# An attention and two gated token-mixing blocks on one core: the planner's constants, its choice rule, buffer counts, and one operation of a decode

## The chip, the cores and the metric

The kernel runs on one core of a Trainium2 chip. The metric is the device time of one execution in microseconds (us). Three runs of the kernel before are given; the profile is of a further execution, with its own time.

## The reference

Three stages follow each other for each of 4 batches (sequence 768, model width 384).

- Attention: 8 heads of width 48. A state of 48x48 per head is multiplied by a gate `f` (a sigmoid of `f_logit`) and takes the outer product of `k` and `v` at each of the 768 tokens; `q` reads it.
- Block 1: `h = gelu(x @ w_in)` with 1024 columns, split in `u` and `v`; `v` is normalised over its columns and scaled by `g_ln`, mixed over the tokens (`w_sg @ v_n + b_sg`), multiplied by `u`, and `x + gated @ w_out` comes out.
- Block 2: `theta = x @ w_theta`; `x cos(theta)` and `x sin(theta)` are mixed over the tokens by `w_tok_r` and `w_tok_i` and added to `x`, which gives `y`; the output is `y + max(y @ w_ch, 0)`.

The weights `w_in`, `w_out`, `w_theta`, `w_tok_r`, `w_tok_i` and `w_ch` arrive as 64-bit floats; `w_sg` and the rest as 32-bit floats.

## The kernel before, in words

**Matmuls.** Every product of block 1 and block 2 is made of three matmuls (`mm3`, L794 to L796): each fp32 operand is split into a high part in the fp32r type and a remainder, and high*high, high*low and low*high are accumulated in one bank of PSUM. `split`, `xsplit` and `load_split` make the parts: ScalarE copies the value into the high part (L803, L813, L454), and VectorE subtracts (L804, L814, L455). Four banks (`mm`) serve the products, two double banks (`at`) the attention.

**Order of the stages.** The attention of batch 0 comes first, in two halves, with nothing dense to run beside it; TensorE is given multiplications with the identity (L1041) to fill its idle time there. Then block 1 of the batches 0 to 3 follows, each beside the attention of the next batch, and then block 2 of batch 3, 0, 1 and 2. In block 1, `p3` mixes over the tokens in all four banks at once (L794 to L796 on `st` and `ar`); at its end VectorE takes the four banks out (L857), multiplies with `u` (L862) and splits.

**The decode (`load_f32`, L417 to L444).** A weight tile of 64-bit floats is loaded as pairs of 32-bit words: into a `raw` buffer (L428) if it is in the background, into an `st` buffer otherwise. ScalarE takes the absolute value of the upper words into a `dt` buffer (L440). VectorE takes the maximum with `TINY` (L441), shifts left by 3 and masks (L442), puts sign and top exponent bit back from the upper word (L443) and the upper bits of the lower word in (L444). `load_split` then splits the `dt` tile: into `win` and `wout`, into `st`, or into a `wt` buffer (L454, L455). 46 tiles are decoded: 12 of `w_in` (256 columns), 4 of `w_out`, and 30 in the background: 24 of `w_tok_r` and `w_tok_i`, 3 of `w_theta`, 3 of `w_ch` (384 columns each). From `wt` a tile is written to a scratch tensor in device memory (L494; L478 for the last six), from which the token-mixing weights are streamed into `st` for each batch (L504, 384 KB) and the channel weights are loaded in one piece into `win` (L486, 1152 KB). A `raw` buffer is free when L444 of its tile is done, a `wt` buffer when its write has landed.

**The attention's output** is copied from PSUM by ScalarE (L744), sent by DMA into `xst` (L767) in pieces of up to 72 KB, and split from there (L813, L814).

**The planner.** All instructions of the main program are put in order before the kernel is built (`Plan.schedule`). Each operation has a due time, a duration and its dependencies; the due time of what feeds it is lowered accordingly (`cost`). The planner then runs a list schedule over the five engines: for each engine it takes the earliest time at which an operation of it could start, looks at all that could start within `LOOK` of that, and picks the one that is due first. Before, a start that was later by some us put `STALL` times as much on its due time. A DMA that is issued at some time is taken to begin moving `ISSUED` later, to move at `RATE` bytes per us behind the DMAs before it, and to have landed `LANDED` after that; the next is not issued until the modelled queue is at most `BACKLOG` us long. The picked order is the order of the instructions on each engine. On the chip each engine runs its instructions in that order, and waits where the data or the buffer isn't there. All DMAs of the main program are issued from SP, in order.

Of the kernel before, what the change touches and what calls it, by code (L numbers as in the profile page):

```python
# [8 lines left out]
F32 = mybir.dt.float32  # L9
# [3 lines left out]
AF = mybir.ActivationFunctionType  # L13
ALU = mybir.AluOpType
# [17 lines left out]
MAGIC = 12582912.0  # L32
TWO_PI = 6.283185
MIN_DECAY = 2.0**-58
TINY = 2.0**-15

N_F = 1
N_SEED = 1
# [8 lines left out]
N_U = 4  # L47
WARM_TO = 100.0
WARM_GAP = 0.3
N_W = 4  # L50
N_DT = 3
N_RAW = 2
N_EARLY = 8
LATE_AT = -6.0
LATE_STEP = 3.3
N_MM = 4
GROUPS0 = [(p, p + 1) for p in range(NP)]
GROUPS1 = GROUPS0
LEAD = 2.0
LATE = 30.0  # L60
HF0, HF1, V_AT, U_AT, DENSE = (-60.0, -40.0), (-25.0, -10.0), -35.0, -27.0, -33.0
ATT_FROM = 0.0
ATT_TO = 100.0
PACE = 1.0
YQ = "SP"
LOOK = 0.15
STALL = 15.0
SWITCH = 2.0
WAIT2 = 0.065

TICK = 10.24 / 3
DMA_SLACK = 1.0
BACKLOG = 2.5
ISSUED = 1.2
LANDED = 0.6
RATE = 335e3
DRAIN = {"PE": 0.0, "DVE": 0.12, "ACT": 0.14, "POOL": 0.05, "SP": 0.0}
LAT = {"PE": 0.21, "DVE": 0.13, "ACT": 0.145, "POOL": 0.1, "SP": 0.0}
SETS = {"G": "gelu_apprx_tanh_and_others", "L": "natural_log_exp_and_others", "S": "silu_and_others"}
# [2 lines left out]
def lat(a, b):  # L82
    if a == b:
        return 0.0
    return 0.21 if a == "PE" else LAT[a] + (0.1 if b == "PE" else 0.0)
# [35 lines left out]
class Plan:  # L121
# [58 lines left out]
    def schedule(self):  # L180
        for o in reversed(self.ops):
            cost = LAT[o.eng] + o.dur + ((ISSUED + LANDED + o.dma / RATE) * DMA_SLACK if o.dma else 0.0)
            for d in o.succ:
# [4 lines left out]
        table, dev, lands = None, 0.0, []  # L188
# [6 lines left out]
        def slot_time(o):  # L195
            t, taken = 0.0, {}
            for b in o.need:
                if b.held:
                    continue
                s = b.slots  # L200
                mine = taken.setdefault(id(s), [])
                at = s.next + len(mine)
                if at >= len(s.order) or s.order[at] is not b:
                    return None
                best = None
                for i in range(s.n):
                    if i in mine:
                        continue
                    prev = s.owner[i]
                    u = 0.0  # L210
                    if prev is not None:
                        for a in prev.acc:
                            if a.end is None:
                                u = None
                                break
                            u = max(u, a.end + (0.0 if a.dma else lat(a.eng, o.eng)))
                    if u is not None and (best is None or u < best[0]):
                        best = (u, i)
                if best is None:
                    return None  # L220
                b.slot = best[1]
                mine.append(best[1])
                t = max(t, best[0])
            return t

        def run(a, dur, left):

            c, i = left / dur, int(a / TICK + 1e-9)
            while left > 1e-6:
                rate = c if ticks.get(i - 1, 0) >= 3060 else c / 2  # L230
                n = min(left, rate * ((i + 1) * TICK - a))
                ticks[i] = ticks.get(i, 0) + n
                left, a, i = left - n, a + n / rate, i + 1
            return a
# [4 lines left out]
        while todo:  # L239
            pick = None  # L240
            for e, c in cand.items():
                best = None
                ready = []
                for o in c:
                    t = o.est
                    if o.need:
                        u = slot_time(o)
                        if u is None:
                            continue
                        t = max(t, u)  # L250
                    t = max(t, free[e])
                    if o.dma and e != "POOL":
                        t = max(t, dev - BACKLOG, lands[-8] if len(lands) >= 8 else 0.0)
                    ready.append((t, o))
                if not ready:
                    continue
                t0 = min(x[0] for x in ready)
                for t, o in ready:
                    if t > t0 + LOOK:
                        continue  # L260
                    vt = o.vt + (SWITCH if self.loads(o, table) else 0.0) + (t - t0) * STALL
                    if best is None or (vt, o.n) < best[0]:
                        best = ((vt, o.n), t, o)
                if pick is None or best[1] < pick[0]:
                    pick = (best[1], best[2])
            t, o = pick
            todo -= 1
            cand[o.eng].remove(o)
            o.need = [b for b in o.need if not b.held]
            for b in o.need:  # L270
                b.held = True
                b.slots.owner[b.slot] = b
                b.slots.next += 1
            if o.eng == "PE" and self.idle and t < WARM_TO and self.quiet(free["PE"]) is not None:
                n, a, bank = 0, free["PE"], self.quiet(free["PE"])
                while True:
                    old = dict(ticks)
                    e = run(a, 0.2145, 512)
                    if e > t - WARM_GAP:
                        ticks.clear()  # L280
                        ticks.update(old)
                        break
                    n, a = n + 1, e
                if n and bank is not None:
                    out.append(((n, bank), None))
            o.start = t
            load, dur = self.loads(o, table), o.dur
            if load:
                table = load
                dur += 1.3  # L290
            if o.eng == "PE":
                dur = run(t, dur, o.cols) - t
            free[o.eng] = o.end = t + dur
            if o.dma:
                dev = max(dev, o.start + ISSUED) + o.dma / RATE
                o.end = dev + LANDED
                if o.eng != "POOL":
                    lands.append(o.end)
            out.append((o, load))
            for d in o.succ:  # L300
                d.left -= 1
                wait = 0.0 if o.dma else lat(o.eng, d.eng) if o.eng != d.eng else DRAIN[o.eng] if o in d.made else 0.0
                d.est = max(d.est, o.end + wait)
                if d.left == 0:
                    cand[d.eng].append(d)
# [27 lines left out]
def body(tc, ctx, att, qkv, flog, w_in, g_ln, w_sgT, b_sg, w_out, w_theta, w_rT, w_iT, w_ch, out):  # L333
    nc = tc.nc
# [41 lines left out]
    def make_state(attention):  # L376
        g = State()
        g.st = Slots(main, "st", N_ST)
        g.w32, g.raw = Slots(main, "wt", N_W), Slots(main, "raw", N_RAW)
        g.dt = Slots(main, "dt", N_DT)  # L380
        g.tmp = Slots(main, "tmp", N_TMP)
# [26 lines left out]
    def dma(pl, eng, nbytes, fn, r=(), w=(), wp=(), vt=None):  # L408
        pl.op(eng, {"SP": 0.43, "ACT": 0.66, "POOL": 1.05}[eng], fn, r, w, wp, dma=nbytes, vt=vt)

    def v2(n):
        return 0.065 + n * 0.00053

    def v1(n):
        return 0.069 + n * 0.00104

    def a1(n):  # L417
        return 0.1 + n * 0.00081

    def load_f32(pl, g, d, src, vt, background=False):  # L420

        n = src.shape[-1]
        get = lambda: d.t[:, :n]
        if src.dtype != I64:
            dma(pl, "SP", n * 512, lambda: nc.sync.dma_start(get(), src), w=[d], vt=vt - 3)
            return
        raw = pl.buf(g.raw if background else g.st, [P, 2 * TH], I32)
        dma(pl, "SP", n * 1024, lambda: nc.sync.dma_start(raw.t[:, : 2 * n], src.bitcast(I32)), [], [raw], vt=vt - 3)  # L428

        def bits():  # L430
            r = raw.t[:, : 2 * n].rearrange("p (n two) -> p n two", two=2)
            return r[:, :, 0], r[:, :, 1]

        def op(dur, fn, eng="DVE"):
            pl.op(eng, dur, fn, [raw], [d], vt=vt)

        V, iget = nc.vector, lambda: get().bitcast(I32)


        op(a1(n), lambda: nc.scalar.activation(get(), bits()[1].bitcast(F32), AF.Abs), "ACT")  # L440
        op(v2(n), lambda: V.tensor_scalar(get(), get(), TINY, None, ALU.max))  # L441
        op(v2(n), lambda: V.tensor_scalar(iget(), iget(), 3, 0x3FFFFFFF, ALU.logical_shift_left, ALU.bitwise_and))  # L442
        op(v1(n), lambda: V.scalar_tensor_tensor(iget(), bits()[1], -0x40000000, iget(), ALU.bitwise_and, ALU.bitwise_or))  # L443
        op(v1(n), lambda: V.scalar_tensor_tensor(iget(), bits()[0], 29, iget(), ALU.logical_shift_right, ALU.bitwise_or))  # L444
# [599 lines left out]
    with tc.manual_schedule():  # L1044
# [19 lines left out]
        def blocks(b, x):  # L1064
            get = lambda pl, i: stream(pl, g, i, pl.vt - LEAD, b == 0 and i < 2 * NS)
            return moe(pl, g, x, get, lambda pl, i: mids[i], out[b], PACE, b == 0)
# [24 lines left out]
        for b in (last, *range(last)):  # L1091
            if b != last:
                x = []
                for hf in range(2):
                    t = pl.buf(g.xst[hf], [P, NK, TH])
# [155 lines left out]
```

## Time and profile before

| | us |
|---|---|
| three runs | 653.91, 655.98, 657.85 |
| median | 655.98 |
| the profiled execution | 658.03 |
| its span, first to last instruction | 656.2 |
| its mean granted clock of TensorE | 0.989 |

The span is what the trace shows; 1.8 us of the profiled execution lie around it. A row of a view of groups ends with the busy time and the mean duration of one instruction. A row of the timeline gives start, duration, engine, line, what it writes and reads, and in brackets how long the engine was idle before it and for whom. The chain of waits is followed back from the last instruction and then printed in order of time.

### The profile page before, as it was taken

The numbers are of one execution on the slowest core, as the hardware profiler recorded it, in microseconds if no ns is written. First come the engines' busy times: TensorE is split into PE (matmuls) and PEld (weight loads), VectorE is DVE, ScalarE is ACT, GpSimd is POOL, SyncE is SP. The second block draws the span as 40 slices with busy tenths as digits, with TensorE's granted clock in tenths as the row PEclk, the third lists the DMA queues.
The fourth block names the chain that finished last, engine by engine and source line by source line (L and its number), as shares of the span: only waits on it lengthen the run. The fifth ranks groups of instructions, "written<-read, shape, count | busy, mean of one in ns | idle before, by whom it ended". The sixth has DMA issues, their size and how long they took to land.

```text
span 656.2 us, 15080 instructions
## 1 busy us (share of the span) xinstructions
PE 616.3 (94%) x6033; PEld 572.8 (87%) x6033; DVE 440.7 (67%) x1030; ACT 353.9 (54%) x752; POOL 20.1 (3%) x32
## 2 busy tenths in 40 slices
PE   9897998798999999999999996989999999999996
PEld 8796887777898888898889996889989999998995
DVE  6898888879878989688786768910771284149203
ACT  6658796656894748954477336700570173029100
POOL 2000010000100001000000000000000000000000
PEclk9997999899999999999999999999999999999998
DMA  9621865387447686483885794298538745860852
GB/s 327 213 92 49 282 223 197 92 295 249 150 144 231 230 267 214 133 262 129 258 287 172 267 311 166 77 333 249 180 112 264 241 133 187 247 204 12 272 186 77
DMA packets 55728, 131.50 MB, mean 200 GB/s; under 512 B 6880, under 2 KB 23264, under 8 KB 55648
## 3 DMA queue, kind: packets, MB, share of 16 engines
q1 hardware_dynamic: 55648, 130.45, 60.1%
q8 instruction: 49, 0.80, 0.5%
q14 instruction: 31, 0.25, 0.1%
HBM read 100.93 MB, written 24.77 MB: 192 GB/s over the span
## 4 chain that ended last, share of the span: by engine, by line
PE 57%; ACT 13%; DMA 13%; DVE 12%; issue 3%; SPq 1%; POOL 0%; ACTq 0%; DVEq 0%; POOLq 0%
PE mm L794 16%; PE mm L796 15%; PE mm L795 15%; DMA xst<-y 3%; PE mm L1041 3%; DMA raw<-in_w_rT 2%; ACT ar L803 2%; DMA raw<-in_w_iT 2%; PE at L733 2%; PE at L651 2%; DMA st<-scratch 2%; DMA scratch<-st 1%; PE at L715 1%; PE at L660 1%; DVE dt L443 1%
## 5 line engine op out<-in xcount | busy, mean ns | idle before, releaser
L794 PE MATMUL mm<-st,ar 128*128 128x384 f32 x480 | 164.1, 342 | 2.3 <-DMA st<-scratch 2.3
L795 PE MATMUL mm<-st,ar 128*128 128x384 f32 x480 | 160.7, 335 | 0.7 <-DVE st L455 0.6
L796 PE MATMUL mm<-st,ar 128*128 128x384 f32 x480 | 160.6, 335 | 0.0
L813 ACT CAST x<-xst 128x384 fp32r<-128x384 f32 x72 | 36.7, 513 | 164.7 <-DVE xst L818 126.8
L818 DVE TENSOR_TENSOR xst<-xst,mm 128x384 f32<-128x384 f32 x48 | 25.9, 552 | 115.9 <-PE mm L796 103.6
L794 PEld LDWEIGHTS mm<-st,ar 128*128 128x128 f32 x480 | 90.1, 188 | 5.3 <-issue 2.6
L795 PEld LDWEIGHTS mm<-st,ar 128*128 128x128 f32 x480 | 90.2, 188 | 1.4 <-DVE st L455 1.4
L796 PEld LDWEIGHTS mm<-st,ar 128*128 128x128 f32 x480 | 90.1, 188 | 0.0
L794 PE MATMUL mm<-x,win 128*128 128x384 f32 x168 | 59.2, 353 | 5.8 <-ACT win L454 4.6
L794 PE MATMUL mm<-win,x 128*128 128x512 f32 (+1 forms) x144 | 56.0, 389 | 8.5 <-DVE tmp L857 3.6
L796 PE MATMUL mm<-x,win 128*128 128x384 f32 x168 | 57.1, 340 | 0.0
L795 PE MATMUL mm<-x,win 128*128 128x384 f32 x168 | 57.0, 339 | 0.0
L796 PE MATMUL mm<-win,x 128*128 128x512 f32 (+1 forms) x144 | 52.7, 366 | 0.0
L795 PE MATMUL mm<-win,x 128*128 128x512 f32 (+1 forms) x144 | 52.6, 365 | 0.0
L803 ACT CAST ar<-tmp 128x384 fp32r<-128x384 f32 x80 | 37.7, 509 | 10.7 <-DVE tmp L862 10.2
L814 DVE TENSOR_TENSOR x<-xst,x 128x384 fp32r<-128x384 f32 x72 | 37.4, 552 | 7.9 <-ACT x L813 6.6
L804 DVE TENSOR_TENSOR ar<-tmp,ar 128x384 fp32r<-128x384 f32 x80 | 41.0, 553 | 0.8 <-ACT ar L803 0.5
L794 PEld LDWEIGHTS mm<-win,x 128*128 128x128 f32 x144 | 27.1, 188 | 14.4 <-DVE tmp L857 5.1
L794 PEld LDWEIGHTS mm<-x,win 128*128 128x128 f32 x168 | 32.2, 192 | 7.1 <-ACT win L454 4.7
L794 PE MATMUL mm<-ar,wout 128*128 128x384 f32 x96 | 34.7, 361 | 3.6 <-ACT u L839 1.9
L1041 PE MATMUL mm<-ident 128*128 128x128 f32 x256 | 34.5, 292 | 1.6 <-POOL ident masks.py:199 1.6
L1041 PEld LDWEIGHTS mm<-ident 128*128 128x128 f32 x256 | 32.4, 205 | 2.2 <-POOL ident masks.py:199 1.6
(137 smaller groups left out, 1153.7 us busy)
## 6 DMA issues: line engine op xcount, KB each, us to landing
st<-scratch SPq DMA_DIRECT2D x132, 384.0 KB, 3.7
qkv<-in_qkv SPq DMA_DIRECT2D x28, 536.0 KB, 4.9
scratch<-wt SPq DMA_DIRECT2D x30, 384.0 KB, 3.7
f<-in_flog SPq DMA_DIRECT2D x6, 768.0 KB, 4.5
scratch<-st SPq DMA_DIRECT2D x12, 384.0 KB, 4.1
raw<-in_w_rT SPq DMA_DIRECT2D x12, 384.0 KB, 3.6
raw<-in_w_iT SPq DMA_DIRECT2D x12, 384.0 KB, 3.7
out<-xst SPq DMA_DIRECT2D x24, 192.0 KB, 1.9
```

What stands on the lines that cost most here:

```text
L443: op(v1(n), lambda: V.scalar_tensor_tensor(iget(), bits()[1], -0x40000000, iget(), ALU.bitwise_and, ALU.bitwise_or))
L651: nc.tensor.matmul(U(c, wide[j]), kt.t[wide[a], i * P + HP * j : i * P + HP * (j + 1)], t.t[wide[a], o : o + D], start=True, stop=True)
L733: nc.tensor.matmul((score if own else apart)(a if own else j, i)[rows[j]], S[c][0]()[rows[j]], Q()[rows[j], tok(i, a)], start=False, stop= ...
L794: nc.tensor.matmul(o, h0, h1, start=start, stop=False)
L795: nc.tensor.matmul(o, h0, l1, start=False, stop=False)
L796: nc.tensor.matmul(o, l0, h1, start=False, stop=stop)
L803: pl.op("ACT", a1(n), lambda: nc.scalar.copy(tiles()[0], src.t[:, :n]), [src], [hi])
L804: pl.op("DVE", v1(n), lambda: V.tensor_sub(tiles()[1], src.t[:, :n], tiles()[0].bitcast(F32)), [src, hi], [lo])
L813: pl.op("ACT", a1(TH), lambda: nc.scalar.copy(X[hf][:, 0, k], T()), [src], [hi])
L814: pl.op("DVE", v1(TH), lambda: V.tensor_sub(X[hf][:, 1, k], T(), X[hf][:, 0, k].bitcast(F32)), [src, hi], [lo])
L818: pl.op("DVE", v1(TH), lambda: V.tensor_add(T(), T(), ps.t[:, :TH]), [ps], [xst[hf].parts[k]])
L1041: nc.tensor.matmul(g.mm.tiles[i][:, :P], ident, ident, start=True, stop=True)
```

## The change

- `RATE`, `ISSUED` and `LANDED` change: a transfer of 384 KB (393,216 bytes) is taken to land after 2.1 + 1.25 + 0.5 = 3.85 us, before after 1.2 + 1.17 + 0.6 = 2.97 us.
[...]
- `STALL` goes, and `LOOK` goes from 0.15 to 0.05 us.
- `wt` buffers go from 4 to 2, `dt` from 3 to 5, `raw` from 2 to 3.
- `LEAD`, by which the due time of a streamed tile lies ahead of its use, goes from 2 to 4 us.

```diff
--- before.py
+++ after.py
@@ -32,7 +32,7 @@
 MAGIC = 12582912.0
 TWO_PI = 6.283185
 MIN_DECAY = 2.0**-58
-TINY = 2.0**-15
+TINY = 2.0**-112
 
 N_F = 1
 N_SEED = 1
@@ -47,33 +47,32 @@
 N_U = 4
 WARM_TO = 100.0
 WARM_GAP = 0.3
-N_W = 4
-N_DT = 3
-N_RAW = 2
+N_W = 2
+N_DT = 5
+N_RAW = 3
 N_EARLY = 8
 LATE_AT = -6.0
 LATE_STEP = 3.3
 N_MM = 4
 GROUPS0 = [(p, p + 1) for p in range(NP)]
 GROUPS1 = GROUPS0
-LEAD = 2.0
+LEAD = 4.0
 LATE = 30.0
 HF0, HF1, V_AT, U_AT, DENSE = (-60.0, -40.0), (-25.0, -10.0), -35.0, -27.0, -33.0
 ATT_FROM = 0.0
 ATT_TO = 100.0
 PACE = 1.0
 YQ = "SP"
-LOOK = 0.15
-STALL = 15.0
+LOOK = 0.05
 SWITCH = 2.0
 WAIT2 = 0.065
 
 TICK = 10.24 / 3
 DMA_SLACK = 1.0
 BACKLOG = 2.5
-ISSUED = 1.2
-LANDED = 0.6
-RATE = 335e3
+ISSUED = 2.1
+LANDED = 0.5
+RATE = 315e3
 DRAIN = {"PE": 0.0, "DVE": 0.12, "ACT": 0.14, "POOL": 0.05, "SP": 0.0}
 LAT = {"PE": 0.21, "DVE": 0.13, "ACT": 0.145, "POOL": 0.1, "SP": 0.0}
 SETS = {"G": "gelu_apprx_tanh_and_others", "L": "natural_log_exp_and_others", "S": "silu_and_others"}
@@ -258,7 +257,7 @@
                 for t, o in ready:
                     if t > t0 + LOOK:
                         continue
-                    vt = o.vt + (SWITCH if self.loads(o, table) else 0.0) + (t - t0) * STALL
+                    vt = o.vt + (SWITCH if self.loads(o, table) else 0.0)
                     if best is None or (vt, o.n) < best[0]:
                         best = ((vt, o.n), t, o)
                 if pick is None or best[1] < pick[0]:
@@ -437,8 +436,7 @@
         V, iget = nc.vector, lambda: get().bitcast(I32)
 
 
-        op(a1(n), lambda: nc.scalar.activation(get(), bits()[1].bitcast(F32), AF.Abs), "ACT")
-        op(v2(n), lambda: V.tensor_scalar(get(), get(), TINY, None, ALU.max))
+        op(a1(n) + 0.03, lambda: nc.scalar.activation(get(), bits()[1].bitcast(F32), AF.Abs, scale=TINY), "ACT")
         op(v2(n), lambda: V.tensor_scalar(iget(), iget(), 3, 0x3FFFFFFF, ALU.logical_shift_left, ALU.bitwise_and))
         op(v1(n), lambda: V.scalar_tensor_tensor(iget(), bits()[1], -0x40000000, iget(), ALU.bitwise_and, ALU.bitwise_or))
         op(v1(n), lambda: V.scalar_tensor_tensor(iget(), bits()[0], 29, iget(), ALU.logical_shift_right, ALU.bitwise_or))
```

## Rows read from the trace of the kernel before

**Rows 1.** Stages: length, busy time and count by engine, TensorE clock, DMA share, GB/s.

```profile
0.00:80.00 80.00, 71.27 (x1092) 64.49 (x1093) 66.67 (x199) 56.58 (x127) 7.07 (x20) 0.96 0.57 197
80.00:440.00 360.00, 337.31 (x3744) 304.75 (x3743) 283.44 (x652) 227.04 (x476) 13.00 (x12) 1.00 0.64 212
440.00:656.00 216.00, 207.69 (x1199) 203.58 (x1198) 90.61 (x180) 70.24 (x150) 0.00 (x0) 0.99 0.57 182
```

**Rows 2.** The first stage, line L1041 alone: the fillers on TensorE.

```profile
0.00:80.00 80.00, 34.46 (x256) 32.41 (x256) 0.96 0.57 197
```

**Rows 3.** Timeline of TensorE: the waits that the sum uses.

```profile
119.49 0.69 PE L794 MATMUL mm<-ar,wout 128*128 128x384 f32 x1 [1.93 <-ACT u L839]
332.85 0.50 PE L794 MATMUL mm<-win,x 128*128 128x512 f32 x1 [1.01 <-DVE tmp L857]
369.64 0.44 PE L794 MATMUL mm<-x,win 128*128 128x384 f32 x1 [1.21 <-DVE tmp L857]
396.97 0.41 PE L794 MATMUL mm<-win,x 128*128 128x384 f32 x1 [2.06 <-issue]
438.55 0.41 PE L794 MATMUL mm<-st,ar 128*128 128x384 f32 x1 [2.31 <-DMA st<-scratch]
```

**Rows 4.** Stages within the start, columns as above.

```profile
36.00:52.00 16.00, 15.64 (x245) 13.71 (x245) 15.75 (x52) 7.97 (x21) 0.00 (x0) 1.00 0.35 114
52.00:61.00 9.00, 4.44 (x62) 3.53 (x62) 7.28 (x29) 8.80 (x22) 0.57 (x1) 0.83 0.09 31
```

**Rows 5.** Timeline of VectorE in the start: the last three maxima there.

```profile
61.49 0.90 DVE L441 TENSOR_SCALAR dt<-dt 128x256 f32<-128x256 f32 x3
```

**Rows 6.** VectorE's maximum at 384 columns: busy and mean, idle before it.

```profile
L441 DVE TENSOR_SCALAR dt<-dt 128x384 f32<-128x384 f32 x34 | 11.8, 355 | 12.8 <-ACT dt L440 12.8
```

**Rows 7.** ScalarE by line: no scale, a scale, a scale and a bias tile.

```profile
L904 ACT ACTIVATE tmp<-tmp 128x384 f32<-128x384 f32 x24 | 12.5, 522 | 1.9 <-DVE tmp L902 1.9
L906 ACT ACTIVATE tmp<-tmp 128x384 f32<-128x384 f32 x24 | 12.6, 525 | 0.7
L905 ACT ACTIVATE tmp<-tmp,halfpi 128x384 f32<-128x384 f32 x24 | 14.5, 602 | 0.0
```

**Rows 8.** The chain of waits where raw loads come late: start, us, what.

```profile
323.80 5.39 DMA raw<-in_w_rT
...
361.50 6.14 DMA raw<-in_w_iT
...
389.74 4.59 DMA raw<-in_w_ch
...
395.78 0.56 DVE dt L443
396.34 2.11 DVE tmp L857 x4
```

**Rows 9.** Timeline of ScalarE: the wait ahead of the table load.

```profile
113.86 0.51 ACT L813 CAST x<-xst 128x384 fp32r<-128x384 f32 x1 [2.74 <-DMA xst<-y]
```

**Rows 10.** The view of DMA issues: count, KB each, median us to landing.

```profile
xst<-y SPq DMA_DIRECT2D x48, 72.0 KB, 3.6
```

**Rows 11.** All loads into the raw tiles.

```profile
DMA to landing us min/median/max: 2.9/4.0/8.8
```

**Rows 12.** Waits of SP's queue: for whom, us in total, times, longest.

```profile
SPq L504 <- PE mm L796: 161.3, 114, 13.7
SPq L428 <- DVE dt L444: 55.7, 24, 7.9
```

**Rows 13.** Timeline of SP's queue: the last raw loads, and the weights' load.

```profile
392.29 0.33 SPq L428 DMA_DIRECT2D raw<-in_w_ch  x1
...
403.19 0.33 SPq L428 DMA_DIRECT2D raw<-in_w_ch  x1
...
430.11 0.59 SPq L486 DMA_DIRECT2D win<-scratch  x1
```

**Rows 14.** Timeline of ScalarE: casts into the wt buffers, closest together.

```profile
224.47 1.34 ACT L454 CAST wt<-dt 128x384 fp32r<-128x384 f32 x3
```

## The prediction

> **What bounds the kernel now.** I read the stages first. TensorE is busy for 337.3 of the 360 us between 80 and 440, and for 207.7 of the last 216 [rows 1]; VectorE there for 283.4 and 90.6. So from 80 us on TensorE is the bound, and all that an edit of the order can win there is its idle time: 22.7 us up to 440, and 8.3 behind, most of it the tail behind the last matmul. The first 80 us are another regime: TensorE looks busy for 71.3 us, but 34.5 of them are fillers [rows 2], so its own work is 36.8 us and 43 us are lost to what it waits for.
>
> Then I looked for what ends TensorE's waits. In the start it is VectorE: 15.75 busy of the 16 us from 36 to 52 [rows 4]. From 52 to 61 it is ScalarE, with 8.80 of 9. After 80 us the waits are single ones of 1 to 2.3 us [rows 3]. The chain of waits says what stands behind three of them: in each, VectorE reached L857, which frees TensorE's four banks, late, because a decode stood in front of it whose raw load had landed late [rows 8]. VectorE waited 12.8 us in all for ScalarE's first step of a decode [rows 6]. The fourth, 1.93 us at 119.49, stands behind a table load on ScalarE, and ScalarE had waited 2.74 us for a piece of attention output [rows 9]. The fifth is a stream that came late at 438.55.
>
> **The change part by part.**
>
> *The maximum.* 46 instructions of L441 go, 34 of them at 0.355 us [rows 6]; the 12 of `w_in` run in the start, where three in a series took 0.90 us [rows 5], so 0.30 each. Of the 12, six lie in the stretch from 36 to 52 us, where VectorE has no gap [rows 4]. In a series the next one overlaps the end of the last, so I take 0.22 for each of these, 1.3 us. Three lie beside ScalarE's stretch from 52 to 61 and are hidden by it. The last three at 61.49 stand before the last parts of `w_in`, but ScalarE feeds them one by one, so I take 0.5 of the 0.90. Sum 1.8 us; the bounds are 0 (ScalarE or the transfers take over at once) and 12 x 0.30 = 3.6. The other 34 run after 80 us, where VectorE is idle for 76.6 of 360 us [rows 1]: each is hidden unless it stands directly before L857; those three are counted below. If this cover were gone, they would be worth 34 x 0.355 = 12.1 us.
>
> *The scale on ScalarE.* 46 instructions get a constant factor. L906, with one, takes 525 ns where L904 takes 522 without [rows 7]: 46 x 3 ns = 0.1 us, off the path. The bounds are 0 and 46 x 80 = 3.7 us, the price of L905, which has a bias tile too; I take the near row, as the change adds no tile.
>
> *The transfer times.* A load of a `raw` tile was planned at 2.97 us (1.2 + 0.6 + 393,216/335,000) and took 5.39, 6.14 and 4.59 before the three waits [rows 8]. It is now planned at 2.1 + 0.5 + 1.25 = 3.85, so the planner places ScalarE's and VectorE's steps 0.88 later, and puts something else in front. The step L441 in the same chains gives 0.36 more. That is 1.24 for each wait, and no more than the wait itself: 1.01 of 1.01, 1.21 of 1.21, 1.24 of 2.06 [rows 3], together 3.5 us. The bounds are 0 and 4.3. A piece of attention output was planned at 1.2 + 0.6 + 0.22 = 2.02 us and took 3.6 [rows 10]; it is now planned at 2.83, so 0.81 of the 1.93 us at 119.49 goes, between 0 and 1.93. All these are waits of engines that run in order: behind L440 ScalarE's casts are queued, behind L441 all of VectorE, and for both TensorE waits.
>
> *The buffers.* The third load of `w_ch` was issued at 403.19, where the second had gone at 392.29 [rows 13]. It waited for a `raw` buffer, that is for an L444, as 24 loads did, for 55.7 us in all [rows 12], with all of SP's queue behind each. It was decoded late, so its write and the load of the whole of `w_ch` at 430.11 fell among the streams of the last stage, and TensorE waited 2.31 us at 438.55 [rows 3]. With a third `raw` buffer and two more `dt` buffers this decode can begin some 10 us earlier and the load is past before the streams start: 2.3 us, between 0 and 2.31. Two `wt` buffers in place of four: the one place in the trace where three casts follow each other is 224.47 [rows 14], for tiles that are needed after 400 us. The cost is 0 there; at the other end a decode that must hold its `dt` for one write of some 4 us, which two more `dt` buffers cover.
>
> *The choice rule and `LEAD`.* Both only reorder. In the last stage the streams wait for TensorE to free their buffer, 161.3 us in 114 issues [rows 12], so an earlier due time moves none. The choice rule is unpriced by any row; I take 0, with the bounds of the rivals below.
>
> Sum: 1.8 + 3.5 + 0.8 + 2.3 = 8.4 us. The profiled execution would go from 658.0 to 649.6. It lies 2.0 above the median of the runs shown, so for the median I say 655.98 - 8.4 = 647.6, rounded 648. By the bounds of the terms, 0 to 3.6 + 4.3 + 1.9 + 2.3 = 12.1, the likeliest case spans 643 to 652.
>
> **The rivals.**
>
> *The waits stay, only the start gains.* A new order is a new list of small mistakes: the raw loads landed between 2.9 and 8.8 us with a median of 4.0 [rows 11], so no constant fits them, and the loads before the three waits were 0.7 to 2.3 us later than even the new 3.85. Then TensorE's 22.7 us of waits come back at other places, and 1.8 us of the start are left, or none: 654. Against it: the plan was wrong in one direction, and the new value is near the median. The Trainium skill, "DMA: Bandwidth & Descriptors", section "Latency and other measured facts", speaks for this rival: it gives the access to device memory as 0.2 us on average and 2 us at high load, so the fixed part of a transfer would follow the load. By that rule the two transfer terms of the sum would be nothing and the rest, 4.1 us, would give 652. The spread of landings in the trace agrees with it.
>
> *Slower: background decodes in front of the urgent operations.* Before, an operation due soon that could start within 0.15 us was waited for; now a decode that can start 0.05 us sooner goes first, whatever its due time. One decode operation takes 0.56 us [rows 8]. The places that it can hurt are those where TensorE waits for a bank or for a theta tile: eight ends of the token mixing and the six theta tiles of the first block 2, 14 in all, at 0.56 each 7.8 us. Less the 1.8 us of the start that is 6 us more: 662. It decides once more than some three of the 14 are hit and the transfer terms don't come. For it: the background work is thick from 300 to 420 us, just where TensorE already waits. Against it: the window is now narrower, which also stops idling for things that are late on the chip, and VectorE has 12 us less to do.
>
> *More than the sum.* If half of the 22.7 us goes (11.4) and the start gives its upper bound (3.6): 641. For it: all five waits have one kind of cause.
>
> **How the numbers follow.** The forecast 0.58; more than the sum 0.11; only the start 0.18; slower 0.13. What can be told from no change is about 0.5%, 3.3 us either way, so faster means below 652.7 and slower above 659.3. Faster: 0.58 + 0.11 and a little of the third case, 0.70; within: 0.17; slower: 0.13. The range for 8 in 10 runs from 640, below the richer case, to 657, which leaves out the slower one and the edge of no change.
>
> **What would show it.** No instruction of the maximum, and VectorE's busy time down by some 13 us; the first dense matmuls some 2 us earlier; L857 no more behind an L440 that waits; TensorE's idle time between 80 and 440 down from 22.7 to about 16; no wait for a stream at 438; the last `w_ch` load next to the second. I am wrong if that idle time stays above 20 us, if SP's waits for L444 grow, or if the two `wt` buffers stop ScalarE's casts before something urgent.

## The result and the profile after

The changed kernel takes 640.18 us (median of 4, 638.33 to 641.33) where the kernel before, run beside it, took 656.91 (653.91 to 659.09): a ratio of 0.9746, 95% interval 0.9698 to 0.9794. The forecast was 648, its range 640 to 657. So the way came out, and the size is about twice what was summed: the time lies 0.2 us inside the lower end of the range, beside the rival "more than the sum" (641 us), which had been given 0.11.

The stages of the changed kernel (length, busy time and count by engine, TensorE clock, DMA share, GB/s), and then TensorE's fillers alone (L1039, which was L1041):

```profile
0.00:80.00 80.00, 72.98 (x1112) 64.98 (x1113) 63.21 (x190) 59.94 (x133) 6.96 (x20) 1.00 0.62 208
80.00:440.00 360.00, 349.49 (x3826) 319.93 (x3825) 265.82 (x621) 227.53 (x477) 13.15 (x12) 0.99 0.68 221
440.00:639.00 199.00, 190.40 (x1102) 186.79 (x1101) 87.56 (x174) 68.72 (x147) 0.00 (x0) 1.00 0.57 178
```

```profile
0.00:80.00 80.00, 34.42 (x260) 32.20 (x260) 1.00 0.62 208
```

Against [rows 1, 2]: in the first 80 us TensorE does 72.98 - 34.42 = 38.56 us of its own work where it did 36.81, so 1.8 us less are idle or filled there. Between 80 and 440 its idle time is 360 - 349.49 = 10.5 us where it was 22.7: 12.2 us. The tail is the same, 8.6 against 8.5 (of the whole span). These make 13.8 of the 17.2 us by which the span went from 656.2 to 639.0. The other 3.4 are TensorE's own busy time (578.4 us without fillers, 581.8 before), for the same products.

What is left of the five waits of the sum [rows 3] in TensorE's timeline of the changed kernel, and, in the last two rows, the two waits beside the first theta tiles that the sum left out:

```profile
116.52 0.69 PE L792 MATMUL mm<-ar,wout 128*128 128x384 f32 x1 [2.38 <-ACT u L837]
...
359.16 0.44 PE L792 MATMUL mm<-x,win 128*128 128x384 f32 x1 [0.81 <-DVE tmp L855]
...
388.97 0.44 PE L792 MATMUL mm<-win,x 128*128 128x384 f32 x1 [0.77 <-DVE tmp L900]
...
392.89 0.44 PE L792 MATMUL mm<-ar,wout 128*128 128x384 f32 x1 [1.74 <-DVE tmp L907]
```

The wait for ScalarE's table load is still there, at 2.38 us in place of 1.93. Of the two behind L857 (now L855) the one of 1.01 is gone and the one of 1.21 is 0.81. The one of 2.06 us ahead of the first theta tile and the one of 2.31 us for a stream are gone. That is 8.5 us down to 3.2, so 5.3 of the 12.2 us; the sum had put 6.6 on these. The other 6.9 came from waits that it had not named: the sum priced five waits, 8.5 of the 22.7 us of idle time.

SP's queue around the last load of the channel weights, SP's waits for the raw buffer (L442 is the last decode step now), VectorE's wait for ScalarE's first decode step, and the landing of all raw loads:

```profile
350.48 0.37 SPq L427 DMA_DIRECT2D raw<-in_w_ch  x1
...
375.14 0.59 SPq L484 DMA_DIRECT2D win<-scratch  x1
```

```profile
SPq L427 <- DVE dt L442: 20.3, 10, 7.6
```

```profile
DVE dt L440 <- ACT dt L439: 3.5, 4, 2.4
```

```profile
DMA to landing us min/median/max: 3.1/4.7/7.4
```

The weights of `w_ch` are loaded at 375, not at 430 [rows 13]; SP's queue stands behind L442 for 20.3 us, not 55.7 [rows 12]; VectorE waits 3.5 us for the first step, not 12.8 [rows 6]. And the raw loads did not get faster: their median is 4.7 us, against 4.0 [rows 11].

In the changed decode VectorE's maximum is gone and ScalarE's absolute value takes a factor of 2^-112. ScalarE's groups: this first decode step in its background form, and the casts into the two `wt` buffers:

```profile
L439 ACT ACTIVATE dt<-raw 128x384 f32<-128x384 f32 x30 | 15.8, 554 | 7.7 <-DMA raw<-in_w_ch 4.0 <-DVE tmp L855 3.3 <-DMA raw<-in_w_iT 0.3
L452 ACT CAST wt<-dt 128x384 fp32r<-128x384 f32 x30 | 14.8, 511 | 10.6 <-DMA scratch<-wt 7.3 <-DVE dt L442 2.2 <-ACT dt L439 0.9
```

The factor costs nothing that shows: 554 ns, against 550 without it. The casts do stand 7.3 us behind writes that have not landed; with the old counts of all three buffers the time is no shorter (below), so this costs nothing that shows.

In the start, from 36 to 52 and from 52 to 61 us, all instructions and then TensorE's fillers alone:

```profile
36.00:52.00 16.00, 15.47 (x269) 12.50 (x265) 15.87 (x55) 10.70 (x27) 0.00 (x0) 1.00 0.39 123
52.00:61.00 9.00, 9.00 (x98) 8.66 (x90) 6.34 (x20) 8.95 (x22) 0.87 (x1) 1.00 0.09 31
```

```profile
36.00:52.00 16.00, 3.60 (x26) 3.13 (x26) 1.00 0.39 123
52.00:61.00 9.00, 6.29 (x54) 6.11 (x54) 1.00 0.09 31
```

Before, there were no fillers from 52 to 61 us, and from 36 to 52 these:

```profile
36.00:52.00 16.00, 7.78 (x63) 7.31 (x62) 1.00 0.35 114
```

VectorE is as full as before from 36 to 52. But TensorE's own work there is 15.47 - 3.60 = 11.87 us, where it was 15.64 - 7.78 = 7.86. From 52 to 61 TensorE looks busy throughout, but 6.29 of the 9.00 us are fillers: its own work is 2.71 us, where it was 4.44 [rows 4]. So own work has moved from ScalarE's stretch into the one before it, and fillers have taken its place.

### The profile page after: what moved, and what is told of

It is laid out like the page before. It is cut to its first block, busy times and chain, and to the rows that moved or that the text cites. A ratio compares the mean times of both kernels' runs of the same rounds, so it can differ in the third digit from the quotient of the medians.

```text
span 639.0 us, 15022 instructions
## 1 busy us (share of the span) xinstructions
PE 612.9 (96%) x6037; PEld 571.7 (89%) x6037; DVE 416.6 (65%) x984; ACT 356.2 (56%) x756; POOL 20.1 (3%) x32
## 4 chain that ended last, share of the span: by engine, by line
PE 76%; ACT 7%; DVE 3%; DMA 1%; issue 1%; SPq 0%; DVEq 0%; ACTq 0%
PE mm L792 23%; PE mm L794 22%; PE mm L793 22%; PE at L731 2%; PE at L713 2%; PE at L649 2%; PE at L637 2%; PE at L658 1%; ACT ar L801 1%; DMA raw<-in_w_ch 1%; ACT tmp L902 1%; ACT tmp L903 1%; DVE tmp L907 1%; ACT L320 1%; ACT tmp L897 1%
## 5 line engine op out<-in xcount | busy, mean ns | idle before, releaser
L792 PE MATMUL mm<-x,win 128*128 128x384 f32 x168 | 58.1, 346 | 0.8 <-DVE tmp L855 0.8
L794 PE MATMUL mm<-x,win 128*128 128x384 f32 x168 | 56.4, 336 | 0.0
L793 PE MATMUL mm<-x,win 128*128 128x384 f32 x168 | 56.3, 335 | 0.0
L792 PE MATMUL mm<-ar,wout 128*128 128x384 f32 x96 | 35.2, 367 | 4.1 <-ACT u L837 2.4
L1039 PE MATMUL mm<-ident 128*128 128x128 f32 x260 | 34.4, 290 | 1.6 <-POOL ident masks.py:199 1.6
L1039 PEld LDWEIGHTS mm<-ident 128*128 128x128 f32 x260 | 32.2, 202 | 2.2 <-POOL ident masks.py:199 1.6
L794 PE MATMUL mm<-ar,wout 128*128 128x384 f32 x96 | 33.1, 345 | 0.0
```

The costliest lines, as they stand in the source:

```text
L792: nc.tensor.matmul(o, h0, h1, start=start, stop=False)
L793: nc.tensor.matmul(o, h0, l1, start=False, stop=False)
L794: nc.tensor.matmul(o, l0, h1, start=False, stop=stop)
L1039: nc.tensor.matmul(g.mm.tiles[i][:, :P], ident, ident, start=True, stop=True)
```

## The experiments

Each ratio is against the kernel before in runs beside it, with its 95% interval. The kernel before was slower beside them (medians of 659.9 to 661.5 us, against 656.9), so ratios are compared; times of kernels only where they ran beside each other.

### One part alone, on the kernel before

**The decode with the order kept.** The maximum isn't issued, the planner still books it:

```diff
-TINY = 2.0**-15
+TINY = 2.0**-112
...
-        op(a1(n), lambda: nc.scalar.activation(get(), bits()[1].bitcast(F32), AF.Abs), "ACT")
-        op(v2(n), lambda: V.tensor_scalar(get(), get(), TINY, None, ALU.max))
+        op(a1(n), lambda: nc.scalar.activation(get(), bits()[1].bitcast(F32), AF.Abs, scale=TINY), "ACT")
+        op(v2(n), lambda: None)
```

> The kernel before with VectorE's maximum gone and the factor on ScalarE, and every instruction else in the order of before: the planner still books the maximum's time. If the maximum's own time is what the change gives (theory 1), the start gains about 1.8 us and three ends of a token mixing 0.36 each: 653 us, 0.4% under before. If the gain is in the order (theory 2), VectorE's saved time becomes idle time: 655 to 657, no difference. VectorE's busy time falls by 13 us or more in both.

Measured: 657.11 us, ratio 0.995 (0.9913 to 0.9986), some 3 us. **The decode alone**, with the planner told of it (the change's lines on the decode, and `TINY`):

> The kernel before with the new decode alone, which the planner knows of, so that it reorders too. Theory 1: as with the order kept, 653 us. Theory 2 (the order decides, and each plan has its own waits): it differs from the run with the order kept by several us either way, 648 to 659.

Measured: 650.67 us, ratio 0.9853 (0.9773 to 0.9933). **The transfer times alone:**

```diff
-ISSUED = 1.2
-LANDED = 0.6
-RATE = 335e3
+ISSUED = 2.1
+LANDED = 0.5
+RATE = 315e3
```

> The kernel before with the new transfer times alone. If the late transfers cost what the prediction put on them, the waits at the ends of the token mixings and behind the table load shrink by 4.3 us: 651 to 652. If the fitted times are the main cause of the whole 17 us, 644 or lower. If waits only move, 656.

Measured: 652.37 us, ratio 0.9882 (0.9811 to 0.9953). **The buffer counts alone:**

```diff
-N_W = 4
-N_DT = 3
-N_RAW = 2
+N_W = 2
+N_DT = 5
+N_RAW = 3
```

> The kernel before with the new buffer counts alone (2 wt, 5 dt, 3 raw). If the third raw buffer takes the last stage's late stream away, 2.3 us less: 653 to 654, and no wait of TensorE for a stream at the start of the last stage. If the buffers are the main cause of the 17 us, 646 or lower. If two wt buffers hold ScalarE's casts, 657 to 660.

Measured: 651.67 us, ratio 0.9871 (0.9787 to 0.9955).

The first run bears out what was put on the maximum itself. Each of the three others gave 7.8 to 9.7 us (its share of 660), where 2.3 to 4.3 had been expected, and their sum, 3.9%, is more than the whole change gives. So two things were open: whether any new order is as good, and what the parts have in common.

**A neutral new order.**

```diff
-WAIT2 = 0.065
+WAIT2 = 0.07
```

> The kernel before with one planned price moved by 5 ns (the planner's second wait of an instruction, 0.065 to 0.07 us), which changes nothing but the order. Theory 2 (any new order of before is several us better or worse, because each has its own chance waits): 646 to 664, clearly away from before on one side. Theory 3 (the parts run alone gain by what they are): within 0.5% of before. If it is about as much faster as the three parts alone were, 1.2 to 1.5%, then those runs show only that the order of before was an unlucky one.

Measured: 660.2 us, ratio 1.0001 (0.9958 to 1.0043). So it isn't enough that the order is new. (The next run, with `LEAD`, is a second new order without a gain.)

**`LEAD` alone:**

```diff
-LEAD = 2.0
+LEAD = 4.0
```

> The kernel before with LEAD 4 in place of 2 alone, the one part not yet run. By the prediction nothing, as before. If it is what all four undone kernels still had in common and so carries the gain: 2% or more under before.

Measured: 660.52 us, ratio 1.0004 (0.9971 to 1.0037). `LEAD` gives nothing.

### Where each part gains

The same three stages of six kernels (columns as above). First the kernel before:

```profile
80.00:200.00 120.00, 111.48 (x1532) 97.42 (x1531) 99.99 (x235) 88.51 (x183) 6.61 (x6) 0.99 0.58 191
200.00:360.00 160.00, 155.12 (x1817) 139.94 (x1816) 129.42 (x304) 103.09 (x219) 6.39 (x6) 1.00 0.67 218
360.00:450.00 90.00, 80.72 (x457) 77.39 (x456) 57.03 (x121) 36.99 (x77) 0.00 (x0) 1.00 0.67 231
```

The neutral order:

```profile
80.00:200.00 120.00, 113.35 (x1518) 98.91 (x1517) 98.62 (x232) 88.94 (x182) 6.61 (x6) 0.94 0.57 188
200.00:360.00 160.00, 155.99 (x1820) 140.41 (x1819) 129.64 (x303) 102.08 (x219) 6.29 (x6) 1.00 0.68 222
360.00:450.00 90.00, 81.89 (x465) 78.78 (x464) 59.68 (x127) 38.02 (x80) 0.00 (x0) 1.00 0.66 230
```

The decode with the order kept, and then the decode alone:

```profile
80.00:200.00 120.00, 112.08 (x1517) 97.42 (x1516) 96.87 (x226) 88.61 (x182) 6.61 (x6) 0.96 0.58 189
200.00:360.00 160.00, 157.43 (x1831) 142.55 (x1830) 126.67 (x290) 103.60 (x222) 6.39 (x6) 1.00 0.68 223
360.00:450.00 90.00, 83.18 (x462) 79.75 (x461) 55.29 (x114) 37.05 (x78) 0.00 (x0) 0.98 0.67 232
```

```profile
80.00:200.00 120.00, 115.01 (x1547) 101.40 (x1546) 100.03 (x233) 89.20 (x184) 6.60 (x6) 0.97 0.59 193
200.00:360.00 160.00, 156.00 (x1815) 139.71 (x1814) 125.37 (x288) 106.34 (x224) 6.33 (x6) 1.00 0.68 223
360.00:450.00 90.00, 86.11 (x493) 83.64 (x492) 51.28 (x105) 35.99 (x75) 0.00 (x0) 1.00 0.71 240
```

The transfer times alone:

```profile
80.00:200.00 120.00, 111.36 (x1510) 97.80 (x1511) 98.76 (x230) 93.31 (x183) 7.15 (x6) 0.93 0.58 190
200.00:360.00 160.00, 159.08 (x1836) 143.51 (x1835) 134.06 (x313) 103.29 (x220) 7.02 (x6) 1.00 0.68 224
360.00:450.00 90.00, 85.61 (x487) 82.80 (x487) 55.05 (x118) 36.74 (x76) 0.00 (x0) 1.00 0.73 245
```

The buffer counts alone:

```profile
80.00:200.00 120.00, 112.11 (x1525) 98.92 (x1524) 99.00 (x239) 89.95 (x186) 6.65 (x6) 0.96 0.58 196
200.00:360.00 160.00, 156.49 (x1817) 140.23 (x1817) 134.49 (x310) 106.71 (x223) 6.16 (x6) 1.00 0.69 222
360.00:450.00 90.00, 87.20 (x500) 84.92 (x499) 53.67 (x114) 35.63 (x75) 0.00 (x0) 1.00 0.67 226
```

TensorE's idle time is the length less its busy time:

| us idle | 80 to 200 | 200 to 360 | 360 to 450 |
|---|---|---|---|
| before | 8.5 | 4.9 | 9.3 |
| neutral order | 6.7 | 4.0 | 8.1 |
| decode, order kept | 7.9 | 2.6 | 6.8 |
| decode alone | 5.0 | 4.0 | 3.9 |
| times alone | 8.6 | 0.9 | 4.4 |
| buffers alone | 7.9 | 3.5 | 2.8 |

The sums, 22.7 before, fall by 9.8, 8.8 and 8.5 us with the decode, the times and the buffers alone, about what they gain. But the neutral order has 3.9 us less idle time too, and gains nothing: its clock is 0.94 in the first stage, and slower products fill the gaps. So the first stage is not to be read by idle time. There I take the moment at which TensorE ends the third of block 1's eight token mixings (the 216th of its matmuls on `st` and `ar`, by its timeline): 203.2 us before, 206.6 with the neutral order, and 202.2, 205.2 and 205.6 with the decode, the times and the buffers alone. No part alone gains there what can be told from a neutral order.

In the second stage, from 200 to 360, the transfer times alone stand out: 0.9 us, against 2.6 to 4.9 in the other five. So it is over all kernels of this document: the seven with the new transfer times have 0.5 to 2.1 us there, the seven with the old ones 2.6 to 5.0. What goes is TensorE's waits for L857 (us in total, times, longest), here before, with the times alone, in the changed kernel, and in that with the old times (L855 where two lines are gone):

```profile
PE mm L794 <- DVE tmp L857: 4.9, 5, 1.3
```

```profile
PE mm L794 <- DVE tmp L857: 0.3, 1, 0.3
```

```profile
PE mm L792 <- DVE tmp L855: 0.8, 1, 0.8
```

```profile
PE mm L792 <- DVE tmp L855: 3.0, 2, 1.5
```

They are at most 1.1 us in the seven kernels with the new times, and 2.3 to 4.9 in the seven with the old. VectorE's own waits for the first decode step (12.8 us before) don't tell the two apart: 6.5 us with the times alone and 3.0 with the buffers alone, where TensorE's second stage gains 4.0 and 1.4.

In the third stage each of the three takes 5 to 6.5 us, and these can be had only once: all kernels with any of the three have 2.8 to 4.5 us there, the four without 6.8 to 9.3 (the neutral order, `LEAD` alone and the decode with the order kept among them). The waits of 1.21 and 2.06 us ahead of the last stage [rows 3] are gone with each of the three, and so is that of 2.31 us for a stream. The last one goes with the load of the whole of `w_ch` (L486, or L485 where a line is gone): it was issued at 430.11 before [rows 13], and in the three runs, in the order above, at

```profile
414.83 0.58 SPq L485 DMA_DIRECT2D win<-scratch  x1
```

```profile
415.75 0.58 SPq L486 DMA_DIRECT2D win<-scratch  x1
```

```profile
405.59 0.58 SPq L486 DMA_DIRECT2D win<-scratch  x1
```

With the order kept it was issued at 428.81, and TensorE's timeline of that run still has the wait for a stream:

```profile
437.89 0.41 PE L794 MATMUL mm<-st,ar 128*128 128x384 f32 x1 [2.37 <-DMA st<-scratch]
```

VectorE's saved time alone does not take that load away from the streams; an order made with it does. Nor was a third `raw` buffer needed for it. With the times alone the last raw load of `w_ch` was issued as late as before (403.19), and the load of the whole still came 14 us earlier:

```profile
403.53 0.33 SPq L428 DMA_DIRECT2D raw<-in_w_ch  x1
```

### One part undone, on the changed kernel

| undone | us | ratio to before |
|---|---|---|
| the decode (maximum back) | 640.77 | 0.9707 (0.9646 to 0.9768) |
| the transfer times | 645.83 | 0.9785 (0.9727 to 0.9842) |
| the buffer counts | 642.05 | 0.9713 (0.9653 to 0.9773) |
| the choice rule | 641.21 | 0.9724 (0.9664 to 0.9783) |
| `LEAD` | 638.85 | 0.9686 (0.9612 to 0.976) |

Each edit is that part of the diff turned round, as here the choice rule:

```diff
-LOOK = 0.05
+LOOK = 0.15
+STALL = 15.0
-                    vt = o.vt + (SWITCH if self.loads(o, table) else 0.0)
+                    vt = o.vt + (SWITCH if self.loads(o, table) else 0.0) + (t - t0) * STALL
```

What was expected, in the order of the table:

> The changed kernel with VectorE's maximum back (the planner books it again). If the parts add (theory 1), it loses what the decode alone gives, 2 to 4 us: 642 to 644. If VectorE's time in the start is the main cause, 648 or more. If the order decides (theory 2), anything from 638 to 650.

> The changed kernel with the old transfer times. Theory 1: it loses 4 to 5 us, 645. If the fitted times are the main cause, 650 or more. If they are no cause, 640.

> The changed kernel with the old buffer counts (4 wt, 3 dt, 2 raw). Theory 1: it loses 2.3 us, 642 to 643, by a late stream at the start of the last stage. If the buffers are the main cause, 648 or more. If they are no cause, 640.

> The changed kernel with the old choice rule (LOOK 0.15, STALL 15). The prediction put nothing on the rule: 640. If the rule is a hidden cause of the gain, 644 or more; if the new rule lets background work in front of urgent work, 637 or less.

> The changed kernel with LEAD back at 2. By the prediction nothing, 640. If LEAD carries the gain, 650 or more. If all parts only help to a point that any four of them reach, 640 to 643.

The changed kernel's own ratio is 0.9746. Four of the five can't be told from it, so none of these four parts is needed once the others are there. The transfer times are: that kernel's runs lay at 645.22 to 646.17, the three that ran beside it at 639.15 to 643.36, 4 to 5 us lower. Its second stage says where:

```profile
200.00:360.00 160.00, 156.59 (x1824) 141.59 (x1823) 128.51 (x309) 108.30 (x230) 6.32 (x6) 1.00 0.73 245
```

The idle time from 200 to 360 us is 3.4 us again, against 160 - 158.52 = 1.5 in the changed kernel, and the other two stages are about as without the undoing (5.5 and 2.9 us, against 6.1 and 2.9).

**The decode and the transfer times together**, on the kernel before, to see whether the gains in different stages add up to the whole:

> The kernel before with the new decode and the new transfer times, and the old rule, LEAD and buffer counts. The decode alone halved TensorE's waits between 60 and 200 us, the times alone took those from 200 to the seventh token mixing, and each took the late channel weights. If these are the shares of the gain and the rest of the change gives nothing: 2.4 to 3% under the before of the same call, about as the whole change. If the gains of single parts are all of one kind and don't combine without the buffers or the rule: 1.5 to 1.9% under it.

Measured: 644.49 us, ratio 0.9753 (0.9701 to 0.9804), which can't be told from the whole change.

```profile
80.00:200.00 120.00, 113.50 (x1593) 99.43 (x1595) 101.46 (x239) 91.42 (x184) 7.13 (x6) 0.97 0.61 203
200.00:360.00 160.00, 159.46 (x1791) 143.92 (x1786) 123.57 (x285) 105.53 (x221) 7.03 (x6) 1.00 0.68 220
360.00:450.00 90.00, 85.55 (x488) 82.90 (x487) 52.09 (x110) 37.03 (x77) 0.00 (x0) 1.00 0.72 242
```

The idle time is 0.5 us in the second stage, as with the transfer times alone, and 4.5 in the third. What the two have over the times alone (652.37 us) comes early: the third token mixing ends at 199.3 us and not at 205.2. That is so in general: it ends between 197.1 and 200.2 us in the seven kernels that have two or three of the parts decode, times and buffers, and between 202.2 and 207.3 in the seven that have one or none. But this is one execution of each, and the granted clock differs between them: up to that moment TensorE was at 1.2 GHz for 6.8 to 13.7 us in the first seven and for 10.2 to 23.9 in the others. With the times alone it was 20.5 us, of which its own products fill 16.6, and with the two together 10.2 and 6.5. At the low clock products of 384 columns follow each other by 0.32 us, at the high one by 0.18 (before, at 61.30 and 64.99 us). So an estimate from these gives the clock some 4.4 of the 5.9 us between the two.

So the gain has three pieces: the second stage, which is the transfer times'; the third, which any of the three parts gives once; and some 3 to 6 us before 200, against the 203.2 of before. That the last takes two of the parts isn't shown, since much of what sets them apart there can be the clock. The rule and `LEAD` aren't needed for any of it, nor, by ratios that overlap, are the buffers beside the other two. No version beat the changed kernel by more than the intervals; the one with `LEAD` at 2 is no worse.

## Why the prediction was right, and where it was half the size

- **The maximum, 1.8 us in the start and three times 0.36.** The size came out and the place did not. 2.9 us were put on it, and with the order kept it gave 0.5% (0.14 to 0.87%) of 660 us. But no run shows 1.8 of them in the start. TensorE's own work (without fillers) in the first 80 us is 36.1 us in that run and 35.3 with the decode alone, against 36.8 before. And the changed kernel with the maximum put back does not lose there what the changed kernel has won (38.6): it has 69.47 - 29.01 = 40.5 us.

```profile
0.00:80.00 80.00, 69.47 (x1063) 61.58 (x1064) 65.85 (x203) 58.25 (x132) 7.04 (x20) 0.96 0.64 216
```

```profile
0.00:80.00 80.00, 29.01 (x210) 27.17 (x210) 0.96 0.64 216
```

  What the start goes with is the transfer times: 38.2 to 40.5 us of own work in the seven kernels with the new ones, 35.3 to 37.1 in the seven with the old. The sum had nothing for them there; by which wait they act in the start was not looked into. Wrong was also the step behind the term: "each is hidden unless it stands directly before L857". It was made for an order that stays. With an order made anew the decode alone gave 1.5%, three times as much; there it also moved the load of `w_ch` from among the streams. VectorE's busy time fell by 24.1 us and not by some 13; with the maximum put back it is still 12 us down, which is the order's.
- **The transfer times, 4.3 us.** Right was that the new times take away TensorE's waits for L857, as the fourteen kernels show. That they do it by planning each load nearer to its landing is not shown: with the times alone the loads landed later too. The term was mis-sized: alone it gave 1.2%, 7.8 us, and undone it costs 4 to 5. I had priced the waits by name, three of them with a raw load behind. The chain has one more of that kind, which I passed over. In the kernel before, a raw load of 5.63 us stood ahead of it in the chain, and TensorE's timeline has the wait:

```profile
203.50 5.63 DMA raw<-in_w_iT
```

```profile
212.36 0.58 PE L715 MATMUL at<-am,qkv 64*64 64x64 f32 x24 [1.01 <-DVE s L697]
```

  It went too, as did that of 1.35 at 242 us behind L857, and that of 1.37 at 327 us behind another instruction of VectorE (L1116). And one that I named stayed: the wait behind the table load, 2.38 us where 1.1 was forecast.
- **The buffers, 2.3 us at 438.** The wait went, but the third `raw` buffer isn't the one reason: the late load of `w_ch` is taken forward by the new buffers, by the decode or by the transfer times, any of them. Undone, the buffers cost nothing that can be told. Most of the 1.3% that they alone give is the 5 to 6.5 us of the third stage that each of the three can have. The three counts were changed together, so what each is worth is not shown.
- **The two waits around the first theta tiles, 1.24 us.** The 2.06 went whole. The waits of 1.25 and 1.70 next to it, which the sum left out, are now 0.77 and 1.74. Before:

```profile
402.24 0.44 PE L794 MATMUL mm<-win,x 128*128 128x384 f32 x1 [1.25 <-DVE tmp L902]
406.16 0.44 PE L794 MATMUL mm<-ar,wout 128*128 128x384 f32 x1 [1.70 <-DVE tmp L909]
```

- **The rule and `LEAD`, nothing.** Right for both, by the two undone and by `LEAD` alone. The rule alone was not run. One reading was wrong and changed nothing: the 161.3 us of SP's waits are the whole run's, and 121.0 of them lie in the last stage.
- **The rivals.** "Background decodes in front of urgent operations" is refuted: with the old rule the time is the same. "The waits stay" is refuted: the neutral order kept the time, the new transfer times did not, though the loads landed still later than the fitted 3.85 us (median 5.1 us with the times alone). The Trainium skill, "DMA: Bandwidth & Descriptors", section "Latency and other measured facts", says that the access to device memory takes longer under load. Before and after agree with that, as the landing went from 4.0 to 4.7 us while the DMA share from 80 to 440 us went from 0.64 to 0.68 [rows 1]; over the other kernels it doesn't hold, as the median is 4.8 us at a share of 0.63 with `LEAD` alone, and 4.1 at 0.67 in the changed kernel with `LEAD` at 2. What I drew from it, that a fitted constant then gains nothing, was wrong. But the plan hardly came nearer to the landings either: at the median it was short by 1.0 us before, by 1.3 with the times alone and by 0.9 in the changed kernel. Why the order made with the longer times keeps decodes from standing in front of L857 stays open. "More than the sum", at 641, is what came, by more than half of the idle time (12.2 of 22.7 us), with 1.8 us in the start where it had 3.6, and by 3.4 us that no term had.

Why the own busy time of TensorE fell by 3.4 us, what the transfer times do in the start, and how the gain before 200 us is made were not settled. Part of the first can be the granted clock: up to 600 us TensorE was at 1.2 GHz for 10.2 us before and for 6.8 after, and half of the difference is 1.7 us. But the clock isn't what makes the gain: the kernel with the maximum put back was at 1.2 GHz for the same 10.2 us as before.

## What to carry to other kernels

In a kernel whose order is made by a planner, price an edit twice: with the order kept, and with the room that it makes given to the planner; here the two were 0.5% and 1.5%. Before terms are added, ask of each wait how many parts of the change would cure it, since it is gained once. And the landing times that a planner assumes are worth a run by themselves: here they gave 7.8 us, where the waits read for them came to 4.3.

## What was not expected of the hardware

The granted clock differs in the first 200 us from one kernel to the next. In the kernel before it was 0.96 over the first 80 us [rows 1], in the neutral order's profile 0.94, in the changed kernel 1.00. These are means of stretches at 2.4 and at 1.2 GHz; before, one at 1.2 began at 58 us:

```profile
58.10:64.80 6.70, 4.31 (x13) 4.31 (x14) 4.76 (x18) 6.67 (x19) 0.86 (x1) 0.50 0.11 38
```

Ahead of it TensorE was busy for 3.93 of the 6 us from 52 to 58, with no filler among its work; the changed kernel has 54 fillers from 52 to 61 us. That goes with the clock in all kernels here: the seven that have fillers (34 to 54) from 52 to 61 us show 1.00 from 52 to 70, and the seven that have none show 0.65 to 0.97 from 52 to 61 and from 61 to 70. The fillers were not varied by themselves.

The times of one kernel spread where the clock falls. All runs of the kernel before but one lay between 653.9 and 664.6 us, the four of the changed kernel between 638.3 and 641.3. That the one causes the other was not tested.
